# The third token tiles of the last two halves multiplied by the output weights as one pair, by Strassen's algorithm

## The chip, the cores and the metric

One core of a Trainium2 chip runs the whole program. The metric is the device time of one execution in microseconds. The kernel before takes 241.07 us as the median of three runs (240.97 to 242.35).

The engines are named as in the profile: PE (TensorE, matrix products; PEld is its loading of weights), DVE (VectorE), ACT (ScalarE), POOL (GpSimd) and SP (SyncE, which here only issues transfers). PE writes its results into eight PSUM banks; DVE and ACT read them out.

## The reference

Attention over 4 batches, 8 heads, 768 positions and 64 numbers per head, with a window of 96 positions, 8 global positions and a bias by distance, and then a feed-forward network with a gate on the 3072 tokens:

```python
scores = scale * q @ k^T + bias;  scores = where(keep, scores, -1e9)
a = exp(scores - max);  a = a / (sum(a) + 1e-09)
x = (a @ v), heads side by side                      # 3072 x 512
gate = maximum(x @ w_gate, 0.0)                      # 512 x 1536
val = x @ w_val                                      # 512 x 1536
out = (gate * val) @ w_out                           # 1536 x 512, float32
```

The kernel computes in bfloat16 with sums in float32.

## The kernel before

The tokens are cut into eight halves, numbered 0 to 7: half a batch each, 384 tokens, as three tiles of 128. For half c the kernel does attention, which gives `xT` (512 x 384), and then the network. Attention of half c + 1 is interleaved with the network of half c, so half 7's network has nothing beside it.

The network of a half is made by `ffn_pieces(c)` as two lists of pieces, each with a weight (about its PE time in microseconds) that serves to space other work. The list `f1` holds 24 products: for each of 12 chunks of the 1536 columns a gate product (`gate`, L521) and a val product (`val`, L528), four matmuls of 384 columns each. ACT applies the maximum (`grelu`, L525) and DVE multiplies val by it into `ht` (L531). `ht` has two buffers, so that of half c stays whole until half c + 2 begins. The list `f2` holds the product with the output weights `wo_sb`. In every half from 1 on:

- The third tile of 128 tokens is multiplied directly (`outp`, L533 to L544): 12 matmuls of 512 columns in four parts of three, a copy by ACT (L543) into a staging tile `osb`, and a store on SP's queue.
- The first two tiles are multiplied together by Strassen's algorithm. Written as a 2 x 2 block matrix, rows being the two tiles and columns the two halves of the 1536 chunks, the left side is multiplied by the 2 x 2 blocks of `wo_sb` in seven products `p4, p3, p1, p2, p5, p6, p7` (in this order) in place of eight. Each product is six matmuls of 256 columns (`block`, L579). The sums of weight blocks are made once (`wo_sum`, L805). The sums of blocks of `ht` are made by DVE in each half: `sum_cb` (for p2 and p5), `sum_ad` (for p1) and `sum_de` (for p6 and p7). Parts of them follow the val products 2, 5, 8, 9 and 10; the last parts stand in `f2`, before its items 2, 3 and 5. The results are put together in the staging tiles: ACT copies p4, p3 and p1; DVE adds and subtracts p2 and p5 in two passes each (L611, L612, L616, L617); p6 and p7 accumulate in the banks of p3 and p1 and take one pass each (L624, L629). Half 7 stores its two tiles in four transfers of half a tile, the others in two whole ones.

The order of all instructions is written out by hand: each engine executes its own in program order. `weave(f_items, *placed)` (L664) issues the pieces of the network one after another and, after each, those other pieces whose place has been passed. `spread` (L659) gives the attention pieces places at equal distances between two fractions of the half's weight: from 0.0 to 0.8 in halves 3 to 6, from 0.07 to 0.82 in half 2, and the preparation of keys and queries of the half after that from 0.25 to 0.75. An attention piece is a group of score products (L397, with ACT's exponential L406 and DVE's masks L359), the product with the values for one head of a pair (`piece_av`, L416, with ACT's logarithm L436 and, after the second head, exponential L441), or the normalization of a pair into `xT` (`piece_norm`, L443, two DVE passes).

From half 1's end on the banks are in two pools: `ff` has three, taken in turn by gate and val products, by the plain tile and by p4, p3 and p1; `x` has five, taken by scores, value products, p2 and p5. A product whose bank has not been read out waits, and all that follows on PE waits with it. At the start of half c from 2 on, `begin` (L546) issues the first gate and val products together, in the order of the parts of `xT`.

Of the kernel before, what the change touches and what calls it, by code (L numbers as in the profile page):

```python
# [8 lines left out]
FP32 = mybir.dt.float32  # L9
BF16 = mybir.dt.bfloat16  # L10
AF = mybir.ActivationFunctionType
ALU = mybir.AluOpType
# [3 lines left out]
def kernel(  # L16
# [12 lines left out]
    nc = tc.nc  # L29
# [14 lines left out]
    NHALF = 2 * B  # L44
# [27 lines left out]
    late = {}  # L72

    PSUM = bass.MemoryType.PSUM
    psum = {}
# [20 lines left out]
    wo_sb = const.tile([128, N_FC, DM], BF16)  # L96
# [408 lines left out]
    out_v = out.rearrange("(s p n) d -> s n p d", p=128, n=NN)  # L505

    begin_of = {}

    def ffn_pieces(c):
        ht = ht_pool.tile([128, N_FC, QH], BF16, name="ht")  # L510
        st = {}
# [38 lines left out]
            if c == 2:  # L550
                product(wg, "g", 1, 0, N_DC - 1)


        N2, D2 = N_FC // 2, DM // 2
        tiles_ = [slice(n * 128, (n + 1) * 128) for n in range(2)]

        def sums_of(name, *shape):
            if name not in st:
                st[name] = late["sums"].tile([128, *shape], BF16, name=name)
            return st[name]  # L560

        cb = lambda: sums_of("cb", N2, 2, 128)
        ad = lambda: sums_of("ad", N2, 128)
        de = lambda: sums_of("de", N_FC, 128)

        def sum_cb(i0, i1):
            nc.vector.tensor_tensor(cb()[:, i0:i1].rearrange("f i n t -> f i (n t)"), ht[:, i0:i1, 0:256],
                                    ht[:, N2 + i0 : N2 + i1, 0:256], op=ALU.add)

        def sum_ad(i0, i1):  # L570
            nc.vector.tensor_tensor(ad()[:, i0:i1], ht[:, i0:i1, tiles_[0]],
                                    ht[:, N2 + i0 : N2 + i1, tiles_[1]], op=ALU.add)

        def sum_de(i0, i1):
            x, y = (1, 0) if i0 < N2 else (0, 1)
            nc.vector.tensor_tensor(de()[:, i0:i1], ht[:, i0:i1, tiles_[x]], ht[:, i0:i1, tiles_[y]],
                                    op=ALU.subtract)

        def block(key, pool, left, right, start, stop):  # L579
            if start:  # L580
                st[key] = psum[pool].tile([128, 512], FP32, name=f"{pool}_ps")
            for i in range(N2):
                nc.tensor.matmul(st[key][:, 0:D2], lhsT=left(i), rhs=right(i),  # L583
                                 start=start and i == 0, stop=stop and i == N2 - 1,
                                 skip_group_check=not start)
            return st[key][:, 0:D2]

        c0, c1 = slice(0, D2), slice(D2, DM)
        bs = lambda name: lambda i: late["bs"][name][:, i]
        V2 = nc.vector.tensor_tensor  # L590

        def store(n, cols, eng=nc.sync):
            eng.dma_start(out=out_v[c, n][:, cols], in_=st["r", n][:, cols])

        def p4():
            for n in range(2):
                st["r", n] = late["osb"].tile([128, DM], FP32, name="osb")
            ps = block("d", "ff", lambda i: ht[:, N2 + i, tiles_[1]], bs("b21-b11"), True, True)
            nc.scalar.copy(st["r", 0][:, c0], ps)

        def p3():
            ps = block("c", "ff", lambda i: ht[:, i, tiles_[0]], bs("b12-b22"), True, True)
            nc.scalar.copy(st["r", 0][:, c1], ps)

        def p1():
            ps = block("a", "ff", lambda i: ad()[:, i], bs("b11+b22"), True, True)
            nc.scalar.copy(st["r", 1][:, c1], ps)

        def p2():
            ps = block("b", "x", lambda i: cb()[:, i, 1], lambda i: wo_sb[:, i, c0], True, True)  # L610
            V2(st["r", 1][:, c0], ps, st["r", 0][:, c0], op=ALU.add)  # L611
            V2(st["r", 1][:, c1], st["r", 1][:, c1], ps, op=ALU.subtract)  # L612

        def p5():
            ps = block("e", "x", lambda i: cb()[:, i, 0], lambda i: wo_sb[:, N2 + i, c1], True, True)
            V2(st["r", 0][:, c1], ps, st["r", 0][:, c1], op=ALU.add)  # L616
            V2(st["r", 0][:, c0], st["r", 0][:, c0], ps, op=ALU.subtract)  # L617
            if c == NHALF - 1:
                store(1, c0)
                store(0, c1)  # L620

        def p6():
            ps = block("c", "ff", lambda i: de()[:, i], bs("b11+b12"), False, True)
            V2(st["r", 1][:, c1], ps, st["r", 1][:, c1], op=ALU.add)  # L624
            store(1, slice(0, DM) if c < NHALF - 1 else c1, nc.sync if c < NHALF - 1 else nc.scalar)

        def p7():
            ps = block("a", "ff", lambda i: de()[:, N2 + i], bs("b21+b22"), False, True)
            V2(st["r", 0][:, c0], ps, st["r", 0][:, c0], op=ALU.add)  # L629
            store(0, slice(0, DM) if c < NHALF - 1 else c0)  # L630

        behind = {2: [lambda: sum_de(0, 3)], 5: [lambda: sum_de(3, 6)], 8: [lambda: sum_cb(0, 3)],
                  9: [lambda: sum_ad(0, 3)], 10: [lambda: sum_de(6, 9)]}

        def val_and_sums(fc):
            val(fc)
            for f in behind.get(fc, ()):
                f()

        begin_of[c] = (begin, lambda: gate(0, N_DC - 1), lambda: val(0, N_DC - 1))  # L640
        f1 = []
        for fc in range(N_FC):
            f1.append((0.65, lambda fc=fc: gate(fc)))
            f1.append((0.65, lambda fc=fc: (val if c < 1 else val_and_sums)(fc)))
        f2 = [(0.65, lambda n=n, part=part: outp(n, part))
              for n in (range(NN) if c < 1 else (NN - 1,)) for part in range(4)]
        if c >= 2:
            f1[:2] = [(1.0, begin_of[c][0]), (0.15, begin_of[c][1]), (0.15, begin_of[c][2])]
        if c == 2:
            f1[0] = (1.5, f1[0][1])  # L650
            f1[3] = (0.15, lambda: gate(1, N_DC - 1))
        if c >= 1:
            f2 += [(0.65, f) for f in (p4, p3, p1, p2, p5, p6, p7)]
            for at, f in ((5, lambda: sum_de(9, 12)), (3, lambda: sum_cb(3, 6)), (2, lambda: sum_ad(3, 6))):
                f2.insert(at, (0.0, f))
        return f1, f2

# [98 lines left out]
    pool = ctx.enter_context(tc.tile_pool(name="late0", bufs=1, side="right", reuse_waits="tile"))  # L756
# [25 lines left out]
    for f in ("m1 g0 m3 v0 m2 g1 K3 K2 m0 g3 K1 S30 S31 g2 K0 S20 v3 S11 v1 S21 A3 N3 v2 S00 S01 "  # L782
              "g5 A2 S10 g4 g6 A0 N2 v5 v4 N0 A1 N1 g7 v7 v6").split():
        i = int(f[1])
# [8 lines left out]
        else:  # L793
# [3 lines left out]
    early.close()  # L797
    ctx.enter_context(open_psum(ff=3, x=5))
    pool = ctx.enter_context(tc.tile_pool(name="late", bufs=1, reuse_waits="tile"))
    late["osb"] = ctx.enter_context(tc.tile_pool(name="osb", bufs=3, reuse_waits="tile"))  # L800
    late["sums"] = ctx.enter_context(tc.tile_pool(name="sums", bufs=1, reuse_waits="tile"))
    late["bs"] = {name: pool.tile([128, N_FC // 2, DM // 2], BF16, name=f"bs{i}")
                  for i, name in enumerate(("b21-b11", "b12-b22", "b11+b22", "b11+b12", "b21+b22"))}

# [39 lines left out]


# [33 lines left out]
```

## Time and profile before

| | |
|---|---|
| median of three runs | 241.07 us (240.97 to 242.35) |
| the profiled execution's own time | 241.74 us |
| its span, from the first to the last instruction | 239.9 us |
| granted TensorE clock, mean | 0.998 |
| PE busy | 233.5 us, 1937 matmuls |
| DVE busy | 173.3 us |
| ACT busy | 153.4 us |
| POOL busy | 85.9 us |
| gate and val products (L518) | 160.9 us of PE |
| plain products with `wo_sb` (L538) | 29.6 us of PE, 112 matmuls of 512 columns |
| network of half 7, its first product to the last pass | 213.69 to 237.08 us |

How to read it: the profile is one execution. "Busy" is the sum of the instructions' lengths in which an engine is at work; matmuls overlap each other, so the distance between the starts of two of them is the time that one takes from PE. In a timeline a line gives the start, the length, the engine, the source line, the operation, output and inputs, the number of instructions that are merged, and in brackets the engine's idle time before them and what ended it.

### The profile page before, as it was taken

The numbers are of one execution on the slowest core, as the hardware profiler recorded it, in microseconds if no ns is written. First come the engines' busy times: TensorE is split into PE (matmuls) and PEld (weight loads), VectorE is DVE, ScalarE is ACT, GpSimd is POOL, SyncE is SP. The second block draws the span as 40 slices with busy tenths as digits, with TensorE's granted clock in tenths as the row PEclk, the third lists the DMA queues.
The fourth block names the chain that finished last, engine by engine and source line by source line (L and its number), as shares of the span: only waits on it lengthen the run. The fifth ranks groups of instructions, "written<-read, shape, count | busy, mean of one in ns | idle before, by whom it ended". The sixth has DMA issues, their size and how long they took to land.

```text
span 239.9 us, 5355 instructions
## 1 busy us (share of the span) xinstructions
PE 233.5 (97%) x1937; PEld 146.6 (61%) x1945; DVE 173.3 (72%) x456; ACT 153.4 (64%) x347; POOL 85.9 (36%) x202
## 2 busy tenths in 40 slices
PE   7899999999999999999999999999999999999994
PEld 3655555665458566666668566676658566676663
DVE  7775955869677788777787687866887677764643
ACT  5897883337775777748774777638774677733330
POOL 6767893208414860903274060902350000000000
PEclk9999999999999999999999999999999999999999
DMA  6999999993976997098519939398431200030003
GB/s 200 181 198 177 257 234 219 185 162 61 270 178 134 301 150 131 8 185 257 108 25 122 285 93 133 19 166 262 67 68 44 90 0 0 3 129 3 4 27 104
DMA packets 69603, 31.42 MB, mean 131 GB/s; under 512 B 47160, under 2 KB 66616, under 8 KB 69576
## 3 DMA queue, kind: packets, MB, share of 16 engines
q0 software_dynamic: 31744, 8.71, 35.3%
q1 hardware_dynamic: 36616, 21.45, 35.1%
q10 hardware_dynamic: 1216, 0.92, 1.2%
q8 instruction: 15, 0.25, 0.4%
q14 instruction: 12, 0.10, 0.1%
HBM read 28.41 MB, written 6.29 MB: 145 GB/s over the span
## 4 chain that ended last, share of the span: by engine, by line
PE 91%; ACT 3%; DVE 2%; issue 1%; ACTq 0%
PE ff_ps L518 53%; PE ff_ps L538 9%; PE ff_ps L583 8%; PE x_ps L427 6%; PE x_ps L397 4%; PE x_ps L583 3%; PE t_ps L459 2%; PE s_ps L341 2%; PE t_ps L272 1%; PE t_ps L682 1%; ACT lnd L436 1%; PE t_ps L310 1%; DVE xT L446 1%; PE s_ps L321 1%; ACT rcp L441 0%
## 5 line engine op out<-in xcount | busy, mean ns | idle before, releaser
L518 PE MATMUL ff_ps<-xT,wg 128*128 128x384 bf16 x384 | 80.7, 326 | 0.5 <-ACT grelu L525 0.4
L518 PE MATMUL ff_ps<-xT,wv 128*128 128x384 bf16 x384 | 80.2, 326 | 0.0
L531 DVE TENSOR_TENSOR ht<-ff_ps,grelu 128x384 bf16<-128x384 f32 x96 | 53.1, 554 | 28.5 <-PE ff_ps L518 13.8
L525 ACT ACTIVATE grelu<-ff_ps 128x384 bf16<-128x384 f32 x96 | 47.1, 492 | 39.4 <-PE ff_ps L518 20.9
L518 PEld LDWEIGHTS <-wg 128*128 128x128 bf16 x384 | 35.9, 98 | 23.9 <-issue 0.9
L518 PEld LDWEIGHTS <-wv 128*128 128x128 bf16 x384 | 36.1, 97 | 23.4 <-issue 1.2
L406 ACT ACTIVATE es<-x_ps 128x360 bf16<-128x360 f32 (+2 forms) x96 | 36.8, 444 | 16.9 <-PE x_ps L397 16.8
L359 DVE TENSOR_TENSOR es<-es,m_all 128x432 bf16<-128x432 bf16 (+4 forms) x108 | 31.2, 334 | 8.2 <-ACT es L406 7.8
L446 DVE TENSOR_TENSOR xT<-x_ps,rcp 64x384 bf16<-64x384 f32 x48 | 26.6, 554 | 9.4 <-ACT rcp L441 8.8
L436 ACT ACTIVATE lnd<-x_ps 64x384 f32<-64x384 f32 x48 | 23.3, 485 | 12.5 <-PE x_ps L427 11.8
L538 PE MATMUL ff_ps<-wo_sb,ht 128*128 128x512 bf16 x112 | 29.6, 379 | 0.4
L363 POOL CAST kqc<-ks 128x384 bf16<-128x384 f32 x24 | 11.6, 532 | 32.3 <-DMA ks<-in_k_dram 32.3
L137 POOL DMA_DIRECT2D vbuf<-in_v_dram x25 | 21.6, 880 | 2.6 <-DMA wv<-in_moe_w_val_dram 2.1
L427 PE MATMUL x_ps<-es,vbuf 128*128 128x216 bf16 (+4 forms) x216 | 21.8, 225 | 0.0
L427 PEld LDWEIGHTS <-vbuf 128*128 128x128 bf16 x216 | 15.8, 97 | 7.7
L538 PEld LDWEIGHTS <-ht 128*128 128x128 bf16 x120 | 10.8, 97 | 9.8 <-issue 0.2
L263 POOL COPY kT<-kqT 128x240 bf16<-128x240 bf16 x16 | 6.9, 430 | 23.0 <-DMA kqT<-kqc 20.5
L363 POOL CAST kqc<-qs 128x384 bf16<-128x384 f32 x24 | 11.6, 522 | 8.1 <-DMA qs<-in_q_dram 8.1
L259 POOL COPY kT<-kqT 128x360 bf16<-128x360 bf16 x10 | 6.0, 604 | 19.9 <-DMA kqT<-kqc 19.9
L441 ACT ACTIVATE rcp<-lnd 128x384 f32<-128x384 f32 x24 | 12.6, 524 | 0.7
L347 ACT ACTIVATE ef<-s_ps 128x720 bf16<-128x720 f32 (+2 forms) x16 | 10.9, 710 | 2.1 <-PE s_ps L341 1.8
L397 PE MATMUL x_ps<-kqT,kT 64*128 64x216 bf16 (+4 forms) x216 | 11.8, 224 | 0.2
(115 smaller groups left out, 252.8 us busy)
## 6 DMA issues: line engine op xcount, KB each, us to landing
out_dram<-osb SPq DMA_DIRECT2D x22, 256.0 KB, 2.7
ks<-in_k_dram SPq DMA_DIRECT2D x6, 768.0 KB, 5.5
qs<-in_q_dram SPq DMA_DIRECT2D x6, 768.0 KB, 12.1
vbuf<-in_v_dram POOLq DMA_DIRECT2D x21, 120.0 KB, 7.9
wg<-in_moe_w_gate_dram POOLq DMA_DIRECT2D x3, 512.0 KB, 7.9
wv<-in_moe_w_val_dram POOLq DMA_DIRECT2D x3, 512.0 KB, 9.8
wo_sb<-in_moe_w_out_dram POOLq DMA_DIRECT2D x1, 1536.0 KB, 19.6
kq<-in_q_dram ACTq DMA_DIRECT2D x2, 192.0 KB, 4.7
```

The costliest lines, as they stand in the source:

```text
L137: nc.gpsimd.dma_start(out=v_dst(b, NG + r0, NG + r0 + n, j), in_=v[b, :, KT * j + r0 : KT * j + r0 + n, :].rearrange("h p d -> p h d"))
L359: nc.vector.tensor_mul(for_all, for_all, mk)
L363: nc.gpsimd.tensor_copy(kqc[:, :, i].rearrange("t n (h d) -> t h n d", d=D)[:, 2 * p : 2 * p + 2], of[s][:, 2 * p : 2 * p + 2, :].rearrang ...
L406: nc.scalar.activation(es[:, e, 0:c], banks[e][:, 0:c], AF.Exp, bias=0.0, scale=scale)
L427: nc.tensor.matmul(av3[:, :, a : a + w], lhsT=vb[:, j, z0 : z0 + 128], rhs=es[:, e, c : c + NN * w].rearrange("k (n p) -> k n p", n=NN), s ...
L436: nc.scalar.activation(ln[o0 : o0 + 64], av[d0 : d0 + 64, 0:QH], AF.Ln, bias=0.0, scale=1.0)
L446: nc.vector.tensor_tensor(xT_of[s][r, p, :], av_of[s, p, e][r, 0:QH], av_of[s, p, "r"][r], op=ALU.mult)
L518: nc.tensor.matmul(st[key][:, 0:QH], lhsT=w_of(w, dc, fc), rhs=xT_of[c][:, dc, :], start=(dc == 0), stop=(dc == N_DC - 1))
L525: nc.scalar.activation(gr, psg[:, 0:QH], AF.Relu, bias=0.0, scale=1.0)
L531: nc.vector.tensor_tensor(ht[:, fc, :], psv[:, 0:QH], st["gr", fc], op=ALU.mult)
L538: nc.tensor.matmul(ps2, lhsT=ht[:, fc, n * 128 : (n + 1) * 128], rhs=wo_sb[:, fc, :], start=(fc == 0), stop=(fc == N_FC - 1))
L583: nc.tensor.matmul(st[key][:, 0:D2], lhsT=left(i), rhs=right(i), start=start and i == 0, stop=stop and i == N2 - 1, skip_group_check=not s ...
```

## The change

The functions of the Strassen product move out of `ffn_pieces` into `strassen(pair, sums)`, which takes any two tiles, each given as half, `ht` and tile number, and the pool for the sums of blocks. Halves 6 and 7 no longer multiply their third tile directly. Half 7 multiplies its own third tile and that of half 6 as one pair, with the tile of half 7 as the first; these seven products stand between half 7's last val product and its old pair. The sums for the new pair come from a pool of their own, `sums3`: `cb3(1)` follows val product 1 of half 7, `ad3` product 6, the first half of `de3` product 7, and `cb3(0)` and the second half of `de3` stand in `f2`.

In half 6 `f2` begins with p4, and the last sums stand before its items 0, 1 and 2; in half 7 the five remaining sums stand before items 0 to 4. The new pair is stored with two whole transfers on SP's queue. The pool of staging tiles has four instead of three.

The fractions for `spread` are multiplied by `part`, which is 22.6 over the half's weight: 22.6 / 22.75 in halves 2 to 5, 22.6 / 20.15 in half 6. The pieces of a half are made before the loads for the half two later are issued.

In the order of instructions this means, besides the new products: in halves 3 to 6 the value product of the second head of pair 2 (and what ACT does with it) comes before the gate product of chunk 11 instead of after it; in half 2 the attention pieces from the masks after pair 1's second score group up to pair 2's value products each come one product earlier. POOL's and SP's orders stay, but for the two stores.

```diff
+    def strassen(pair, sums):
+        N2, D2 = N_FC // 2, DM // 2
+        st = {}
+        last = pair[0][0] == NHALF - 1 and pair[0][2] == 0
+        def h(i, f0, f1):
+            _, ht, n = pair[i]
+            return ht[:, f0:f1, n * 128 : (n + 1) * 128]
...
+        def sum_cb_of(i):
+            V2(cb()[:, :, i], h(i, 0, N2), h(i, N2, N_FC), op=ALU.add)
+        def sum_ad(i0, i1):
+            V2(ad()[:, i0:i1], h(0, i0, i1), h(1, N2 + i0, N2 + i1), op=ALU.add)
+        def sum_de(i0, i1):
+            x, y = (1, 0) if i0 < N2 else (0, 1)
+            V2(de()[:, i0:i1], h(x, i0, i1), h(y, i0, i1), op=ALU.subtract)
...
+        def p4():
+            for i in range(2):
+                st["r", i] = late["osb"].tile([128, DM], FP32, name="osb")
+            ps = block("d", "ff", lambda i: h(1, N2 + i, N2 + i + 1)[:, 0], bs("b21-b11"), True, True)
+            nc.scalar.copy(st["r", 0][:, c0], ps)
...
+        return sum_cb, sum_cb_of, sum_ad, sum_de, [(0.65, f) for f in (p4, p3, p1, p2, p5, p6, p7)]
+    PAIRED = (6,)
+    third_of = {}
...
+        plain = range(NN) if c < 1 else () if c - c % 2 in PAIRED else (NN - 1,)
+        sum_cb, _, sum_ad, sum_de, products = strassen([(c, ht, 0), (c, ht, 1)], "sums")
         behind = {2: [lambda: sum_de(0, 3)], 5: [lambda: sum_de(3, 6)], 8: [lambda: sum_cb(0, 3)],
                   9: [lambda: sum_ad(0, 3)], 10: [lambda: sum_de(6, 9)]}
+        rest = (lambda: sum_ad(3, 6), lambda: sum_cb(3, 6), lambda: sum_de(9, 12))
+        if c in PAIRED:
+            third_of[c] = ht
+        elif c - 1 in PAIRED:
+            _, cb3, ad3, de3, products3 = strassen([(c, ht, NN - 1), (c - 1, third_of[c - 1], NN - 1)], "sums3")
+            behind[1] = [lambda: cb3(1)]
+            behind[6] = [lambda: ad3(0, N_FC // 2)]
+            behind[7] = [lambda: de3(0, N_FC // 2)]
+            rest = (lambda: cb3(0), lambda: de3(N_FC // 2, N_FC)) + rest
...
         if c >= 1:
-            f2 += [(0.65, f) for f in (p4, p3, p1, p2, p5, p6, p7)]
-            for at, f in ((5, lambda: sum_de(9, 12)), (3, lambda: sum_cb(3, 6)), (2, lambda: sum_ad(3, 6))):
+            f2 += (products3 if c - 1 in PAIRED else []) + products
+            places = (2, 3, 5) if plain else (0, 1, 2) if c in PAIRED else (0, 1, 2, 3, 4)
+            for at, f in list(zip(places, rest))[::-1]:
                 f2.insert(at, (0.0, f))
...
-    late["osb"] = ctx.enter_context(tc.tile_pool(name="osb", bufs=3, reuse_waits="tile"))
+    late["osb"] = ctx.enter_context(tc.tile_pool(name="osb", bufs=4, reuse_waits="tile"))
     late["sums"] = ctx.enter_context(tc.tile_pool(name="sums", bufs=1, reuse_waits="tile"))
+    late["sums3"] = ctx.enter_context(tc.tile_pool(name="sums3", bufs=1, reuse_waits="tile"))
...
     for c in range(2, NHALF):
+        f1, f2 = ffn_pieces(c)
+        part = 22.6 / sum(t for t, _ in f1 + f2)
...
-            placed.append(spread(attention_pieces(c + 1), *((0.07, 0.82) if c == 2 else (0.0, 0.8))))
+            placed.append(spread(attention_pieces(c + 1), *((0.07, 0.82 * part) if c == 2 else (0.0, 0.8 * part))))
...
-            placed.append(spread(early_pieces(c + 2), 0.25, 0.75))
-        f1, f2 = ffn_pieces(c)
+            placed.append(spread(early_pieces(c + 2), 0.25 * part, 0.75 * part))
         weave(f1 + f2, *placed)
```

More of the change, by code (lines that the diff above doesn't have):

```diff
@@ L507, with sums_of, sum_cb, block @@
     begin_of = {}
+    c0, c1 = slice(0, DM // 2), slice(DM // 2, DM)
+    V2 = nc.vector.tensor_tensor
+    def strassen(pair, sums):
[5 more added lines that the diff above has]
+            return ht[:, f0:f1, n * 128 : (n + 1) * 128]
+        def sums_of(name, *shape):
+            if name not in st:
+                st[name] = late[sums].tile([128, *shape], BF16, name=name)
+            return st[name]
+        cb = lambda: sums_of("cb", N2, 2, 128)
+        ad = lambda: sums_of("ad", N2, 128)
+        de = lambda: sums_of("de", N_FC, 128)
+        def sum_cb(i0, i1):
+            ht = pair[0][1]
+            V2(cb()[:, i0:i1].rearrange("f i n t -> f i (n t)"), ht[:, i0:i1, 0:256],
+               ht[:, N2 + i0 : N2 + i1, 0:256], op=ALU.add)
+        def sum_cb_of(i):
[5 more added lines that the diff above has]
+            V2(de()[:, i0:i1], h(x, i0, i1), h(y, i0, i1), op=ALU.subtract)
+        def block(key, pool, left, right, start, stop):
+            if start:
+                st[key] = psum[pool].tile([128, 512], FP32, name=f"{pool}_ps")
+            for i in range(N2):
+                nc.tensor.matmul(st[key][:, 0:D2], lhsT=left(i), rhs=right(i),
+                                 start=start and i == 0, stop=stop and i == N2 - 1,
+                                 skip_group_check=not start)
+            return st[key][:, 0:D2]
+        bs = lambda name: lambda i: late["bs"][name][:, i]
+        def store(i, cols, eng=nc.sync):
+            c, _, n = pair[i]
+            eng.dma_start(out=out_v[c, n][:, cols], in_=st["r", i][:, cols])
+        def p4():
[3 more added lines that the diff above has]
+            nc.scalar.copy(st["r", 0][:, c0], ps)
+        def p3():
+            ps = block("c", "ff", lambda i: h(0, i, i + 1)[:, 0], bs("b12-b22"), True, True)
+            nc.scalar.copy(st["r", 0][:, c1], ps)
+        def p1():
+            ps = block("a", "ff", lambda i: ad()[:, i], bs("b11+b22"), True, True)
+            nc.scalar.copy(st["r", 1][:, c1], ps)
+        def p2():
+            ps = block("b", "x", lambda i: cb()[:, i, 1], lambda i: wo_sb[:, i, c0], True, True)
+            V2(st["r", 1][:, c0], ps, st["r", 0][:, c0], op=ALU.add)
+            V2(st["r", 1][:, c1], st["r", 1][:, c1], ps, op=ALU.subtract)
+        def p5():
+            ps = block("e", "x", lambda i: cb()[:, i, 0], lambda i: wo_sb[:, N2 + i, c1], True, True)
+            V2(st["r", 0][:, c1], ps, st["r", 0][:, c1], op=ALU.add)
+            V2(st["r", 0][:, c0], st["r", 0][:, c0], ps, op=ALU.subtract)
+            if last:
+                store(1, c0)
+                store(0, c1)
+        def p6():
+            ps = block("c", "ff", lambda i: de()[:, i], bs("b11+b12"), False, True)
+            V2(st["r", 1][:, c1], ps, st["r", 1][:, c1], op=ALU.add)
+            store(1, c1 if last else slice(0, DM), nc.scalar if last else nc.sync)
+        def p7():
+            ps = block("a", "ff", lambda i: de()[:, N2 + i], bs("b21+b22"), False, True)
+            V2(st["r", 0][:, c0], ps, st["r", 0][:, c0], op=ALU.add)
+            store(0, c0 if last else slice(0, DM))
+        return sum_cb, sum_cb_of, sum_ad, sum_de, [(0.65, f) for f in (p4, p3, p1, p2, p5, p6, p7)]
@@ L551, in begin @@
                 product(wg, "g", 1, 0, N_DC - 1)
[L554 to L630, printed above, removed]
+        plain = range(NN) if c < 1 else () if c - c % 2 in PAIRED else (NN - 1,)
+        sum_cb, _, sum_ad, sum_de, products = strassen([(c, ht, 0), (c, ht, 1)], "sums")
         behind = {2: [lambda: sum_de(0, 3)], 5: [lambda: sum_de(3, 6)], 8: [lambda: sum_cb(0, 3)],
@@ L645, in ffn_pieces @@
         f2 = [(0.65, lambda n=n, part=part: outp(n, part))
-              for n in (range(NN) if c < 1 else (NN - 1,)) for part in range(4)]
+              for n in plain for part in range(4)]
         if c >= 2:
```

## The prediction, made before the changed kernel was run

> **What bounds the kernel now.** I read the page from the top. The first fence holds the span, the busy times and the chain that ended last, by engine and by line.
>
> ```profile
> span 239.9 us, 5355 instructions
> ...
> PE 233.5 (97%) x1937; PEld 146.6 (61%) x1945; DVE 173.3 (72%) x456; ACT 153.4 (64%) x347; POOL 85.9 (36%) x202
> ...
> PE 91%; ACT 3%; DVE 2%; issue 1%; ACTq 0%
> PE ff_ps L518 53%; PE ff_ps L538 9%; PE ff_ps L583 8%; PE x_ps L427 6%; PE x_ps L397 4%; PE x_ps L583 3%; PE t_ps L459 2%; PE s_ps L341 2%; PE t_ps L272 1%; PE t_ps L682 1%; ACT lnd L436 1%; PE t_ps L310 1%; DVE xT L446 1%; PE s_ps L321 1%; ACT rcp L441 0%
> ```
>
> PE is the bound: 97% busy, 91% of the chain. So a product that goes is worth its PE time, and a wait that PE gets is paid in full. VectorE (DVE) has 28% spare on the mean, but the change works on the ends of two halves, so next I read the timeline there. The end of the kernel (start, length, engine, line, operation, count):
>
> ```profile
> 229.28 2.75 PE L538 MATMUL ff_ps<-wo_sb,ht 128*128 128x512 bf16 x11
> ...
> 231.88 1.47 PE L583 MATMUL ff_ps<-bs,ht 128*128 128x256 bf16 x12
> ...
> 233.19 0.82 PE L583 MATMUL ff_ps<-bs,ad 128*128 128x256 bf16 x6
> ...
> 233.84 1.47 PE L583 MATMUL x_ps<-wo_sb,cb 128*128 128x256 bf16 x12
> ...
> 235.15 1.47 PE L583 MATMUL ff_ps<-bs,de 128*128 128x256 bf16 x12
> ...
> 236.66 0.42 DVE L629 TENSOR_TENSOR osb<-ff_ps,osb 128x256 f32<-128x256 f32 x1 [0.16 <-PE ff_ps L583]
> ```
>
> Lengths overlap; the distance between starts is the cost. A plain tile (12 matmuls of 512 columns; one record is missing) takes 231.88 - 229.28 = 2.60 us, 0.217 each. Six matmuls of 256 columns take 233.84 - 233.19 = 0.65 us, 0.109 each; a Strassen pair (seven such products) takes 4.58.
>
> The same place in half 6, with the other engines:
>
> ```profile
> 204.23 0.83 ACT L406 ACTIVATE es<-x_ps 128x360 bf16<-128x360 f32 x2
> ...
> 205.15 0.49 ACT L525 ACTIVATE grelu<-ff_ps 128x384 bf16<-128x384 f32 x1
> ...
> 205.25 0.81 PE L518 MATMUL ff_ps<-xT,wv 128*128 128x384 bf16 x4
> 205.66 0.48 ACT L436 ACTIVATE lnd<-x_ps 64x384 f32<-64x384 f32 x1
> ...
> 205.90 1.46 PE L538 MATMUL ff_ps<-wo_sb,ht 128*128 128x512 bf16 x5
> 206.17 0.56 DVE L531 TENSOR_TENSOR ht<-ff_ps,grelu 128x384 bf16<-128x384 f32 x1 [0.78 <-ACT lnd L436]
> 206.17 0.52 ACT L441 ACTIVATE rcp<-lnd 128x384 f32<-128x384 f32 x1
> 206.65 0.59 DVE L359 TENSOR_TENSOR es<-es,m_all 128x384 bf16<-128x384 bf16 x2
> ...
> 207.15 1.12 DVE L446 TENSOR_TENSOR xT<-x_ps,rcp 64x384 bf16<-64x384 f32 x2
> ...
> 208.30 0.36 DVE L571 TENSOR_TENSOR ad<-ht 128x384 bf16<-128x384 bf16 x1
> ...
> 208.58 0.55 DVE L567 TENSOR_TENSOR cb<-ht 128x768 bf16<-128x768 bf16 x1
> ...
> 213.31 0.42 DVE L624 TENSOR_TENSOR osb<-ff_ps,osb 128x256 f32<-128x256 f32 x1
> ...
> 214.01 0.49 PE L518 MATMUL ff_ps<-xT,wv 128*128 128x384 bf16 x2
> ```
>
> To see: the last chunk of ht (206.17 to 206.73) and both sums (to 209.13) are done before PE reaches the Strassen products at 209.10 to 211.7, because the plain tile stands in between (205.90 to 209.10, with two attention pieces of 0.31 each). The pass of p6 (213.31 to 213.73) frees the bank that half 7's first val product takes at 214.01: 0.3 us of slack. The plain tile is cover for DVE, and half 6 loses it.
>
> **Part 1, the arithmetic on PE.** Two plain tiles go: 205.90 to 209.10 less 0.62 of attention, 2.58, and 2.60. One Strassen pair comes: 4.58. Sum **-0.60 us**. That needs weight loads that stay hidden, 42 in place of 24 and 0.098 each: the row shows 12 loads and 12 matmuls in 1.31 us, so they are.
> The Trainium skill, "TensorE: Matmul & The Clock Gate", section "The mechanism", says the contrary in one place, that a weight load overlaps a running matmul only when the row groups differ; here all loads fill the whole array. By it the pair would cost 42 x 0.207 = 8.7 us against 24 x 0.315 = 7.6, +1.1 in place of -0.60; the 0.109 us between starts disagrees, and I keep the row.
>
> **Part 2, the end of half 6.** In the new order v11, the last val product, is followed at once by p4, whose sixth matmul reads the last chunk of ht. Also the factor on the attention positions moves one attention product (second head of pair 2) ahead of the last gate product, so ACT gets its logarithm and exponential ahead of the last grelu. I work it through from the rows' starts; PE is unchanged up to 205.90.
> - ACT: es to 205.06, logarithm to 205.57, exponential to 206.08, grelu to 206.57. Before, it was done at 205.64.
> - DVE: the last ht chunk then runs 206.60 to 207.15 instead of 206.17 to 206.73.
> - PE: p4's sixth matmul would start at 205.90 + 5 x 0.109 = 206.45; with 0.2 for the release and the load (an estimate) it starts at 207.35: **+0.90**. p3 ends at 208.11, attention at 208.42, p1 at 209.07, attention at 209.38.
> - DVE, in the new order and at the row's distances: masks to 207.65, ad to 207.93, normalization of pair 2 (1.15) to 209.08, cb to 209.63, de to 210.0. p2 wants cb's second half at 209.71 and gets it at 209.83: **+0.12**.
> - p2 ends at 210.16, its two DVE passes run to about 211.1; the normalization of pair 3 stands next in DVE's queue (1.13) to 212.2, the two passes of p5 to 212.9, that of p6 to 213.3. PE has finished p7 at 212.12 and half 7's first gate product at 212.45; the val product waits for the bank of p6 until about 213.35: **+0.90**.
> So half 7's first val product comes at 213.35 instead of 214.01, 0.66 earlier, where without stalls it would be 2.58 earlier. Stalls together **+1.92**. Bounds: 0.45 from below, if grelu keeps its old time: ht ends at 206.73 and p4 waits 0.45, while DVE's work from there to p6's pass, 6.2 us without a pause, ends at 212.4 and the bank is in time; 0 if PE reaches p4 that much later than I have it; and 2.6 if each of the three releases takes 0.2 more. I take 1.9, since every duration in the chain is from a row.
>
> **Part 3, the end of half 7.** Seven more products stand there: 9.16 in place of 2.60 + 4.58, +1.98; this is already in the sum of part 1. The first four read half 6's ht and sums made behind products 1, 6 and 7, so the last ht chunk has 2.6 us. The new sums are five, of 768 elements each; the nearest row, cb, is 0.55, bounds 0.36 and 1.12 (ad; the pair of normalizations). In half 7 DVE is busy 11.95 of 23.2 us and a chunk period of 1.30 us holds 0.56 + 0.55. At the tail cb3's first half is needed 2.6 us after v11 and comes at 1.4; p6' and p7' free their banks at about 4.9 and 5.3, wanted at 5.2 and 5.9. Cost 0, up to 0.5 if the sums take 1.12. ACT does three copies of 0.37 for the plain copy of 0.57, and idles here. The two whole stores go to SP's queue some 3 us ahead of the last three, about the 2.7 us in which such a store lands: 0, up to 0.3. The last pass and store stay as they are.
>
> **Part 4, the rest.** The fourth staging tile takes away a wait for a store's landing that no row shows: 0. In halves 3 to 5 the late grelu delays the last chunk by 0.4 to 0.6 us, under the cover of the plain tile: 0. In half 2 some fifteen attention pieces come one product (0.65) earlier; there one score group takes 0.67 at 87.98 where others take 0.48, a wait of 0.2 for a bank that may go, and new ones may come: -0.2 to +0.6, taken as 0. Moving the halves' piece construction ahead of the loads changes nothing in SP's or GpSimd's order: 0.
>
> **Sum.** -0.60 + 1.92 = +1.32 us. Against the profiled execution's own 241.74 (span 239.9 and 1.8 around it) this is 243.1; that execution lies 0.67 over the median 241.07, so for the median 242.4. About 1% is what a measurement of this kernel can tell from no change, and this is 0.55%.
>
> **Rivals.**
> - Gain kept: ACT or DVE reach the releases in time and only part 1 is left, -0.6 to +0.1: 240.5 to 241.2. For it: DVE's 28% spare. Against: p4's sixth matmul cannot start before the last ht chunk, and with the trace's own 206.73 it is late. The other side is decided at the val bank: under 0.6 us of stalls in all, the kernel is faster. 0.22.
> - More stalls: half 2's earlier pieces meet banks not yet free (three later score groups, 0.2 to 0.4 each) or the tail of half 7 falls behind (0.5 to 0.8), 0.5 to 1.6 on top of the forecast: 242.9 to 244.0. For it: 87.98. Against: the same pieces at the same distance in halves 3 to 5 show no such wait. 0.18.
> - The change does not do what it says: the pair is more PE time than two tiles, 244. Against: 0.109 and 0.217. 0.03, within the last.
>
> **How the numbers follow.** Forecast 0.60, its own range 241.4 to 243.1. With the rivals the range is 240.3 to 243.5, which leaves out the edges of both. Faster by over 1% (under 238.7) has no mechanism: 0.02. Slower by over 1% (over 243.5) is half of the second rival: 0.09. Within 1%: 0.89.
>
> **What the changed profile would show.** Right: an idle of about 0.9 us within or behind p4 in half 6, with the last ht as releaser; the val product of half 7 starting some 0.7 us before 214.01, after an idle released by p6's pass; no idle among half 7's fourteen products. Wrong: the first val at 211.5 (gain kept), or PE idle in half 2. Wrong altogether if the products' distance is not 0.109.

## The result, and the profile after

The changed kernel takes 243.71 us (median of six runs, 243.25 to 244.33), the kernel before 241.56 us (six runs, 240.97 to 242.35). The ratio is 1.009, with a 95% interval of 1.0067 to 1.0114, that is +1.6 to +2.75 us. The forecast was 242.4 us, +1.32 over the median of before as it was then known (241.07). The direction was right and the time lies 0.2 us above the range, which ended at 243.5.

The profiled execution after takes 244.33 us, 2.59 more than that of before, at the same mean clock (0.998). Its page, in the first lines and the chain that ended last:

```profile
span 242.6 us, 5413 instructions
...
PE 234.3 (97%) x1963; PEld 148.0 (61%) x1963; DVE 176.8 (73%) x467; ACT 153.1 (63%) x348; POOL 85.9 (35%) x202
...
PE 77%; DMA 8%; DVE 5%; ACT 5%; issue 2%; POOL 1%; ACTq 0%
PE ff_ps L614 48%; PE ff_ps L551 9%; PE ff_ps L634 6%; PE x_ps L427 5%; DMA wv<-in_moe_w_val_dram 4%; DMA wg<-in_moe_w_gate_dram 4%; PE x_ps L397 4%; PE x_ps L551 3%; ACT lnd L436 2%; DVE xT L446 1%; PE t_ps L711 1%; ACT grelu L621 1%; DVE ht L627 1%; ACT es L406 1%; PE t_ps L459 1%
```

PE's arithmetic went down and its busy time didn't (234.3 against 233.5): the trace of before lacks eight matmuls (L538 has 112 records of 120). So the busy time can't show a gain of 0.6 us; distances between starts can. The chain now has 5% each of DVE and ACT, and among its lines are `grelu` (L621) and `ht` (L627), which the lines listed before did not have. Its 8% of DMA lies ahead of 28.6 us, in the transfers of the first weights (`wv`, `wg`), of which more below.

The waits of PE and of its weight loads name some that the trace of before doesn't have (engine, waiting line, what it waited for: us in total, times, longest). First the weight loads:

```profile
PEld L551 <- DVE ht L627: 0.8, 1, 0.8
...
PEld L427 <- DVE es L359: 0.7, 3, 0.3
...
PEld L397 <- DVE xT L446: 0.3, 1, 0.3
```

Then PE itself:

```profile
PE ff_ps L614 <- DVE osb L591: 0.8, 1, 0.8
PE ff_ps L551 <- DVE ht L627: 0.5, 1, 0.5
```

The `ht` and `osb` lines are the two large stalls of the prediction's part 2. The three of L427 on `es` are not in the prediction; the one of L397 on `xT` lies in half 2, where it had allowed for one. The timeline of half 6's end after the change (start, length, engine, line, operation, count):

```profile
206.64 0.48 ACT L436 ACTIVATE lnd<-x_ps 64x384 f32<-64x384 f32 x1
...
207.46 0.71 PE L551 MATMUL ff_ps<-bs,ht 128*128 128x256 bf16 x5
207.58 0.47 ACT L621 ACTIVATE grelu<-ff_ps 128x384 bf16<-128x384 f32 x1
208.09 0.56 DVE L627 TENSOR_TENSOR ht<-ff_ps,grelu 128x384 bf16<-128x384 f32 x1 [1.14 <-ACT grelu L621]
...
208.70 0.94 PE L551 MATMUL ff_ps<-bs,ht 128*128 128x256 bf16 x7 [0.54 <-DVE ht L627]
...
212.08 1.47 PE L551 MATMUL ff_ps<-bs,de 128*128 128x256 bf16 x12
212.35 1.12 DVE L446 TENSOR_TENSOR xT<-x_ps,rcp 64x384 bf16<-64x384 f32 x2
...
214.17 0.42 DVE L591 TENSOR_TENSOR osb<-ff_ps,osb 128x256 f32<-128x256 f32 x1
...
214.64 0.48 PE L614 MATMUL ff_ps<-xT,wv 128*128 128x384 bf16 x2 [0.76 <-DVE osb L591]
```

To see: p4 starts at 207.46; its sixth matmul would start at 207.46 + 5 x 0.109 = 208.00 and starts at 208.70, after the last chunk of `ht` (208.09 to 208.65). Half 7's first val product could start 0.33 after its first gate product (213.39), at 213.72, and starts at 214.64: the pass of p6 (L591) that frees its bank stands in DVE's queue behind the normalization of 212.35 and p5's two passes. The end of the kernel:

```profile
229.91 1.47 PE L551 MATMUL ff_ps<-bs,ht 128*128 128x256 bf16 x12
...
234.49 1.47 PE L551 MATMUL ff_ps<-bs,ht 128*128 128x256 bf16 x12
...
237.77 1.47 PE L551 MATMUL ff_ps<-bs,de 128*128 128x256 bf16 x12
...
239.28 0.42 DVE L596 TENSOR_TENSOR osb<-ff_ps,osb 128x256 f32<-128x256 f32 x1 [0.16 <-PE ff_ps L551]
```

The two pairs follow each other at 4.58 us, without a wait.

Where the 2.6 us between the spans lie (239.94 and 242.56 us), from the starts of the same gate and val products in the two traces:

| stretch | after minus before, us |
|---|---|
| start to half 0's ninth product (a wait for the first weights) | +0.52 |
| half 2 | +0.20 |
| halves 3, 4, 5 | +0.27, +0.25, +0.31 |
| half 6 up to p4 (before: the plain tile's start) | 0.00 |
| from there to half 7's first val product: 7.18 against 8.11 | -0.93 |
| first val product to the last pass: 24.64 against 22.65 | +1.99 |
| behind the last pass | 0.0 |

The first row is not the change's: the profiled executions of eight kernels with the same start differ there by up to 1.64 us (below). Without it the rows give +2.1, which agrees with the difference of the medians, +2.15.

In these two traces 0.83 us come from halves 3 to 5, where the change does nothing but move places by 0.7%. Half 3 shows how. Before (timeline around its last products):

```profile
122.89 0.44 PE L427 MATMUL x_ps<-es,vbuf 128*128 128x216 bf16 x4
...
123.08 0.49 ACT L525 ACTIVATE grelu<-ff_ps 128x384 bf16<-128x384 f32 x1
...
123.60 0.48 ACT L436 ACTIVATE lnd<-x_ps 64x384 f32<-64x384 f32 x1
...
124.08 0.56 DVE L531 TENSOR_TENSOR ht<-ff_ps,grelu 128x384 bf16<-128x384 f32 x1 [0.74 <-ACT lnd L436]
...
124.55 0.64 DVE L359 TENSOR_TENSOR es<-es,m_all 128x432 bf16<-128x432 bf16 x2
...
125.10 0.43 PE L427 MATMUL x_ps<-es,vbuf 128*128 128x216 bf16 x4
...
125.38 0.81 PE L538 MATMUL ff_ps<-wo_sb,ht 128*128 128x512 bf16 x3
```

After:

```profile
122.95 0.43 PE L427 MATMUL x_ps<-es,vbuf 128*128 128x216 bf16 x4
...
123.74 0.48 ACT L436 ACTIVATE lnd<-x_ps 64x384 f32<-64x384 f32 x1
...
124.25 0.52 ACT L441 ACTIVATE rcp<-lnd 128x384 f32<-128x384 f32 x1
...
124.68 0.47 ACT L621 ACTIVATE grelu<-ff_ps 128x384 bf16<-128x384 f32 x1
...
125.19 0.56 DVE L627 TENSOR_TENSOR ht<-ff_ps,grelu 128x384 bf16<-128x384 f32 x1 [0.94 <-ACT grelu L621]
...
125.66 0.59 DVE L359 TENSOR_TENSOR es<-es,m_all 128x432 bf16<-128x432 bf16 x2
...
125.82 0.71 PE L427 MATMUL x_ps<-es,vbuf 128*128 128x216 bf16 x4
...
126.09 0.11 PEld L427 LDWEIGHTS <-vbuf 128*128 128x128 bf16 x2 [0.17 <-DVE es L359]
...
126.37 0.81 PE L634 MATMUL ff_ps<-wo_sb,ht 128*128 128x512 bf16 x3
```

To see: before, the last `grelu` runs at 123.08, ahead of the logarithm; after, the logarithm and the exponential (`rcp`) go first, and `grelu` runs at 124.68. The last chunk of `ht` comes at 125.19 instead of 124.08. The whole half starts 0.72 us later in the second trace (first gate product at 105.33 instead of 104.61), so the chunk itself is 0.39 late. The masks (`es`) of pair 3 stand behind it in DVE's queue. The value product that needs these masks stands inside the plain tile. Before, it went through without a wait (start 125.10, the plain tile goes on at 125.38: 0.28). After, it starts at 125.82 and the plain tile goes on at 126.37: 0.55, so +0.27. The plain tile covers the late chunk of `ht`, as predicted; it does not cover what is queued behind that chunk.

In half 2 a score group of pair 3 meets a bank whose two readers (the normalization of pair 1) have just begun. The timeline there, after:

```profile
93.47 1.13 DVE L446 TENSOR_TENSOR xT<-x_ps,rcp 64x384 bf16<-64x384 f32 x2
...
93.53 0.86 PE L397 MATMUL x_ps<-kqT,kT 64*128 64x216 bf16 x10
...
94.06 0.11 PEld L397 LDWEIGHTS <-kT 64*128 64x128 bf16 x3 [0.30 <-DVE xT L446]
```

The same group took 0.48 at 93.85 before; it takes 0.86 now. The group at 87.98, 0.67 before, takes 0.48 now. That is about +0.4 and -0.2, the half's +0.20. It is not clear of chance: with the old order half 2 takes 27.72 us in the trace of before and 27.96 in that of e3 (last section), and 27.91 here.

### The profile page after: what moved, and what is told of

It is laid out like the page before. It is cut to its first block, busy times and chain, and to the rows that moved or that the text cites. A ratio compares the mean times of both kernels' runs of the same rounds, so it can differ in the third digit from the quotient of the medians.

```text
span 242.6 us, 5413 instructions
## 1 busy us (share of the span) xinstructions
PE 234.3 (97%) x1963; PEld 148.0 (61%) x1963; DVE 176.8 (73%) x467; ACT 153.1 (63%) x348; POOL 85.9 (35%) x202
## 4 chain that ended last, share of the span: by engine, by line
PE 77%; DMA 8%; DVE 5%; ACT 5%; issue 2%; POOL 1%; ACTq 0%
PE ff_ps L614 48%; PE ff_ps L551 9%; PE ff_ps L634 6%; PE x_ps L427 5%; DMA wv<-in_moe_w_val_dram 4%; DMA wg<-in_moe_w_gate_dram 4%; PE x_ps L397 4%; PE x_ps L551 3%; ACT lnd L436 2%; DVE xT L446 1%; PE t_ps L711 1%; ACT grelu L621 1%; DVE ht L627 1%; ACT es L406 1%; PE t_ps L459 1%
## 5 line engine op out<-in xcount | busy, mean ns | idle before, releaser
L627 DVE TENSOR_TENSOR ht<-ff_ps,grelu 128x384 bf16<-128x384 f32 x96 | 53.2, 555 | 29.3 <-PE ff_ps L614 12.7
L621 ACT ACTIVATE grelu<-ff_ps 128x384 bf16<-128x384 f32 x96 | 47.1, 492 | 39.4 <-PE ff_ps L614 19.9
L359 DVE TENSOR_TENSOR es<-es,m_all 128x432 bf16<-128x432 bf16 (+4 forms) x108 | 30.4, 328 | 8.2 <-ACT es L406 7.8
L634 PE MATMUL ff_ps<-wo_sb,ht 128*128 128x512 bf16 x96 | 24.2, 379 | 0.0
L427 PE MATMUL x_ps<-es,vbuf 128*128 128x216 bf16 (+4 forms) x216 | 22.4, 225 | 0.2
L427 PEld LDWEIGHTS <-vbuf 128*128 128x128 bf16 x216 | 15.9, 97 | 7.9 <-DVE es L359 0.7
L634 PEld LDWEIGHTS <-ht 128*128 128x128 bf16 x96 | 8.6, 97 | 7.9 <-issue 0.2
L551 PE MATMUL ff_ps<-bs,ht 128*128 128x256 bf16 x96 | 12.0, 273 | 0.5 <-DVE ht L627 0.5
L259 POOL COPY kT<-kqT 128x360 bf16<-128x360 bf16 x10 | 5.5, 554 | 19.0 <-DMA kqT<-kqc 19.0
```

What stands on the lines that cost most here:

```text
L359: nc.vector.tensor_mul(for_all, for_all, mk)
L427: nc.tensor.matmul(av3[:, :, a : a + w], lhsT=vb[:, j, z0 : z0 + 128], rhs=es[:, e, c : c + NN * w].rearrange("k (n p) -> k n p", n=NN), s ...
L621: nc.scalar.activation(gr, psg[:, 0:QH], AF.Relu, bias=0.0, scale=1.0)
L627: nc.vector.tensor_tensor(ht[:, fc, :], psv[:, 0:QH], st["gr", fc], op=ALU.mult)
L634: nc.tensor.matmul(ps2, lhsT=ht[:, fc, n * 128 : (n + 1) * 128], rhs=wo_sb[:, fc, :], start=(fc == 0), stop=(fc == N_FC - 1))
```

## The experiments

Two questions were open. Is it the shifted places alone that cost time in halves 2 to 5, and by which engine? And what sets the stalls at the end of half 6: the late chunk of `ht`, or DVE's queue? The kernel before was run beside them: 241.53 us (median of 27 runs) beside the first four, 241.52 (29 runs) beside the last four.

| kernel | median us | ratio to before, 95% |
|---|---|---|
| changed kernel | 243.71 | 1.009 (1.0067 to 1.0114) |
| e1_new_places_only | 242.53 | 1.0046 (1.003 to 1.0063) |
| e2_old_places | 242.21 | 1.0038 (1.0023 to 1.0053) |
| e3_p3_first | 242.27 | 1.0027 (1.0011 to 1.0042) |
| e4_norm_last | 241.34 | 0.9999 (0.9983 to 1.0015) |
| e5_late_log | 241.71 | 1.0002 (0.999 to 1.0014) |
| e6_norm_only | 241.78 | 1.0007 (0.9995 to 1.0019) |
| e7_two_pairs | 242.28 | 1.003 (1.0017 to 1.0044) |
| e8_three_pairs | 242.97 | 1.0056 (1.0042 to 1.0071) |

For the kernels that differ at the end of half 6, the traces give these distances (us):

| kernel | half 6's first product with `wo_sb` or its sums, to half 7's first val product | from there to the last pass | sum, against before |
|---|---|---|---|
| before | 8.11 | 22.65 | 0 |
| changed kernel | 7.18 | 24.64 | +1.06 |
| e2_old_places | 6.82 | 24.64 | +0.70 |
| e3_p3_first | 6.82 | 24.64 | +0.70 |
| e6_norm_only | 5.90 | 24.92 | +0.06 |
| e4_norm_last | 5.52 | 24.96 | -0.28 |

### The new places alone

The kernel before with the new fractions and nothing else:

```diff
     for c in range(2, NHALF):
+        part = 22.6 / 22.75
...
-            placed.append(spread(attention_pieces(c + 1), *((0.07, 0.82) if c == 2 else (0.0, 0.8))))
+            placed.append(spread(attention_pieces(c + 1), *((0.07, 0.82 * part) if c == 2 else (0.0, 0.8 * part))))
...
-            placed.append(spread(early_pieces(c + 2), 0.25, 0.75))
+            placed.append(spread(early_pieces(c + 2), 0.25 * part, 0.75 * part))
```

> The kernel before, with one edit: the fractions of the attention places times 22.6/22.75, so that its order in halves 2 to 5 is that of the changed kernel; no new pair. Theory A (the places cost time by themselves: in each half the late grelu delays the last ht chunk, DVE's masks queue behind it, and the value product of the last pair waits for them, 0.27 us a half in halves 3 to 6, and 0.2 in half 2): +1.3 us over the kernel before. Theory B (the places are harmless, the whole loss is at the ends of halves 6 and 7 and in memory layout or startup): 0.

Measured: 242.53 us, ratio 1.0046 (1.003 to 1.0063), +1.0 us by the medians. In the trace half 2 is 0.20 longer, halves 3, 4 and 5 are longer by 0.28, 0.41 and 0.27, and half 6, which keeps its plain tile here, by 0.22. The three waits of the value product's weight loads on the masks are there again (0.8 us in total). The stretches add up to 1.4, more than the medians show; half 4's part is 0.41 here and 0.25 in the changed kernel, whose order there is the same. So about half of the loss needs no Strassen product at all.

### The old places in the changed kernel

```diff
-        part = 22.6 / sum(t for t, _ in f1 + f2)
+        part = 22.74 / sum(t for t, _ in f1 + f2)
```

> The changed kernel with 22.74 for 22.6, so that its order up to half 6's last val product is that of the kernel before; the new pair stays. Theory A: halves 2 to 5 fall back to the times of before and the last ht chunk of half 6 comes 0.4 us earlier, so +0.7 us over the kernel before in place of the changed kernel's +2.15. Theory B: only half 6 gains by the earlier chunk, some 0.4, so +1.7.

Measured: 242.21 us, ratio 1.0038 (1.0023 to 1.0053). Halves 2, 3 and 5 take their old time, half 4 0.16 us less, and what is left, +0.70 in the table of distances, is the end of half 6 against the arithmetic. With `grelu` back at its old place p4's wait shrinks from 0.70 to 0.34 (sixth matmul at 207.78, p4 from 206.90). The wait for p6's bank stays at 0.92 (half 7's first gate product at 212.47, its first val product at 213.72 instead of 0.33 after it). So that wait does not come from the late chunk of `ht`.

### p3 ahead of p4

e2 with the first two products of half 6's pair exchanged, in the same banks. p3 reads the first six chunks of `ht`, so the last chunk gets 0.65 us more.

```diff
-            if start:
+            if start and key not in st:
...
+        def p4_tiles():
+            for i in range(2):
+                st["r", i] = late["osb"].tile([128, DM], FP32, name="osb")
+            st["d"] = psum["ff"].tile([128, 512], FP32, name="ff_ps")
...
+            (lambda: (p4_tiles(), p3()), p4, p1, p2, p5, p6, p7) if pair[0][0] in PAIRED else
+            (p4, p3, p1, p2, p5, p6, p7))]
```

> As the run with the old places, and in half 6 p3 is multiplied before p4, into the same banks as before, so that the last ht chunk is needed 0.65 us later. Theory A1 (behind the wait in p4 stands DVE's queue, which sets when half 7's first val product gets its bank): the wait in p4 goes, but comes back at p2 or at the bank; +0.7, no gain over the run with the old places. Theory A2 (each wait is paid by itself): the 0.4 us of p4's wait is gained, +0.3.

Measured: 242.27 us, ratio 1.0027 (1.0011 to 1.0042), and in the trace the same 6.82 us as e2. p4's wait is gone, and p2 waits in its place. The timeline (the first two lines are p2, the last is half 7's first val product):

```profile
208.98 0.49 PE L551 MATMUL x_ps<-wo_sb,cb 128*128 128x256 bf16 x3
...
209.68 1.16 PE L551 MATMUL x_ps<-wo_sb,cb 128*128 128x256 bf16 x9 [0.20 <-DVE cb L534]
...
213.23 0.48 PE L621 MATMUL ff_ps<-xT,wv 128*128 128x384 bf16 x2 [0.76 <-DVE osb L596]
```

p2's fourth matmul would start at 208.98 + 3 x 0.109 = 209.31 and starts at 209.68: 0.37 late, as much as p4 had been in e2 (0.34 there, 0.03 at p2). So the waits ahead of p2 don't add up. DVE's queue decides when p2 can run, and a product moved ahead of it only moves the idle time. The bank wait did not change.

### DVE's order at the end of half 6

e3 with the second half of `cb` ahead of pair 2's normalization, and pair 3's normalization behind the pass of p6:

```diff
-        N = lambda p: [(0.0, lambda: piece_norm(s, p))]
+        N = lambda p: [(0.0, lambda: piece_norm(s, p) if s - 1 not in PAIRED or p < HP - 1 else None)]
...
-            places = (2, 3, 5) if plain else (0, 1, 2) if c in PAIRED else (0, 1, 2, 3, 4)
+            places = (2, 3, 5) if plain else (0, 0, 2) if c in PAIRED else (0, 1, 2, 3, 4)
...
+        if c in PAIRED:
+            f2.insert(-1, (0.0, lambda: piece_norm(c + 1, HP - 1)))
```

> As the run with p3 first, and in half 6 DVE's order is changed: the last cb sum before the normalization of pair 2, and the normalization of pair 3 behind the pass of p6 instead of before the passes of p5. Theory A1 (DVE's queue, with the 1.1 us normalization in front of the pass that frees the bank, makes the wait of half 7's first val product): that wait goes to about 0.2 us, later at the last part of xT; -0.3 us against the kernel before. Theory A2 (the waits stand alone): the bank's wait of 0.8 goes, -0.4 against the kernel before; told from A1 by the run with p3 first. If neither moves the time, the loss isn't at this place: +0.7.

Measured: 241.34 us, ratio 0.9999 (0.9983 to 1.0015). It is 2.4 us under the changed kernel and can't be told from the kernel before. The timeline of the same place:

```profile
210.32 0.41 DVE L596 TENSOR_TENSOR osb<-ff_ps,osb 128x256 f32<-128x256 f32 x1
...
210.65 1.11 DVE L446 TENSOR_TENSOR xT<-x_ps,rcp 64x384 bf16<-64x384 f32 x2
210.65 0.49 PE L621 MATMUL ff_ps<-xT,wg 128*128 128x384 bf16 x2
...
210.98 0.49 PE L621 MATMUL ff_ps<-xT,wv 128*128 128x384 bf16 x2
...
211.82 0.32 PE L621 MATMUL ff_ps<-xT,wg 128*128 128x384 bf16 x1
...
212.27 0.81 PE L621 MATMUL ff_ps<-xT,wg 128*128 128x384 bf16 x4
```

The pass of p6 now runs at 210.32 and the val product follows its gate product at once. All stalls up to there are gone: 5.52 us, where the kernel before less the plain tile gives 8.11 - 2.58 = 5.53. Still the whole stretch is only 0.28 us shorter than before, not 0.60. The rest went into the first products of half 7. From the first val product to the next chunk's gate product (212.27) it takes 1.29 instead of 0.98 (214.01 to 214.99 before): the last part of `xT` is now made at 210.65 to 211.76, just when these products want it, and p7's pass stands behind it.

### The logarithm behind grelu

e1 (new places, plain tiles) with ACT's order alone put back: the logarithm and exponential of pair 2's second head are issued behind the last `grelu`. PE and DVE keep e1's order.

```diff
+        if p == 3 and g == 2 and s in later:
+            later.pop(s)()
...
+        def on_act():
+            nc.scalar.activation(ln[o0 : o0 + 64], av[d0 : d0 + 64, 0:QH], AF.Ln, bias=0.0, scale=1.0)
+            if e == 1:
+                av_inverse(s, p, ln)
+        if e == 1 and p == 2 and s >= 3:
+            later[s] = on_act
+        else:
+            on_act()
...
```

> As the run with the new places only, and ACT's logarithm and exponential for pair 2 (after its second value product) issued behind the last grelu, where they stood before; PE's and DVE's orders stay as with the new places. Theory A (the late grelu is the cause: chunk, masks, value product in turn): in halves 3 to 5 the 0.27 us a half and in half 6 as much go, and half 2's 0.2 stays: +0.2 us over the kernel before. Theory B (the earlier value product on PE costs by itself): +1.1 as with the new places.

Measured: 241.71 us, ratio 1.0002 (0.999 to 1.0014). Halves 3 to 6 take the old time again; half 2, where this edit leaves the order as it is in e1, keeps +0.20. No wait of a value product on masks is left. Half 3's timeline:

```profile
124.03 0.49 ACT L538 ACTIVATE grelu<-ff_ps 128x384 bf16<-128x384 f32 x1 [0.36 <-PE ff_ps L531]
...
124.54 0.48 ACT L439 ACTIVATE lnd<-x_ps 64x384 f32<-64x384 f32 x1
...
124.75 0.56 DVE L544 TENSOR_TENSOR ht<-ff_ps,grelu 128x384 bf16<-128x384 f32 x1 [0.66 <-PE ff_ps L531]
...
125.77 0.44 PE L429 MATMUL x_ps<-es,vbuf 128*128 128x216 bf16 x4
```

`grelu` is back ahead of the logarithm, `ht` comes 0.39 earlier than in the changed kernel (124.75 against 125.19, less the 0.05 by which half 3 starts earlier here), and the value product takes its 0.44 without a pause. This settles the cause in halves 3 to 5: two ACT instructions, 1.0 us long, ahead of one `grelu` cost a quarter to 0.4 of a microsecond in each half.

### The normalization alone

e2 with only pair 3's normalization moved behind the pass of p6; p4 stays first and `cb` where it was.

```diff
+        N = lambda p: [(0.0, lambda: piece_norm(s, p) if s - 1 not in PAIRED or p < HP - 1 else None)]
...
+        if c in PAIRED:
+            f2.insert(-1, (0.0, lambda: piece_norm(c + 1, HP - 1)))
```

> As the run with the old places, with one edit: the normalization of pair 3 in half 6 behind the pass of p6 on DVE. Theory A1: the 0.8 us wait of half 7's first val product goes, less 0.2 for the last part of xT, and p4's wait of 0.2 to 0.45 stays: +0.1 us over the kernel before. If the wait has another cause: +0.7 as with the old places.

Measured: 241.78 us, ratio 1.0007 (0.9995 to 1.0019). The bank wait is gone and p4's stays. The table of distances gives 0.92 less up to the first val product, and 0.28 given back in half 7, as in e4. So the bank wait was made by one normalization (two DVE passes, 1.11 us together) that stood ahead of the pass that frees the bank.

### More pairs

If the pair gains in e4's order, more third tiles might be joined: e4 with two pairs, and with three.

```diff
-    PAIRED = (6,)
+    PAIRED = (4, 6)
```

> As the run with the normalization last, with halves 4 and 5 paired too. If the arithmetic is worth 0.6 us a pair and the order at the end of an even half costs 0.3 of it: -0.5 us against the kernel before. Rival: half 5 has attention beside it, and its 14 products with five more sums and six more passes on DVE (about 4.9 us) make new waits: 0 to +0.5.

```diff
-    PAIRED = (4, 6)
+    PAIRED = (2, 4, 6)
```

> As before with halves 2 and 3 paired as well: by the arithmetic -0.8 us against the kernel before; by the rival +0.3 to +1.

Measured: 242.28 and 242.97 us, ratios 1.003 and 1.0056. Each further pair costs 0.7 to 0.95 us instead of gaining 0.6. The timeline of half 5's end in the kernel with two pairs:

```profile
181.15 1.12 DVE L446 TENSOR_TENSOR xT<-x_ps,rcp 64x384 bf16<-64x384 f32 x2
...
182.48 0.81 PE L551 MATMUL ff_ps<-bs,ht 128*128 128x256 bf16 x6 [0.46 <-ACT osb L571]
...
183.34 0.42 DVE L596 TENSOR_TENSOR osb<-ff_ps,osb 128x256 f32<-128x256 f32 x1
...
183.81 0.82 PE L551 MATMUL ff_ps<-bs,ad 128*128 128x256 bf16 x6 [0.52 <-DVE osb L596]
```

Fourteen products follow each other there with half 6's attention beside them. The second pair's p3 starts when ACT has copied p4 of the same pair (L571, 182.06 to 182.43), and its p1 when the pass of the first pair's p6 (L596) has freed a bank. From start to start, with 0.65 for a product, p3 is 0.63 late (its p4 starts at 181.20) and p1 0.68. A normalization stands ahead of the passes again. Half 7, which has no attention beside it, shows no such wait. Halves 4 and 5 together take 55.42 us, 0.73 more than in the kernel before; with the 0.60 that the pair saves, their stalls are 1.33, and these two make 1.31 of it. In the kernel with three pairs halves 4 and 5 take 0.78 more than before and halves 2 and 3 0.46; by which waits is open.

## Why the prediction was right and wrong

**The step that failed** is in part 4: "In halves 3 to 5 the late grelu delays the last chunk by 0.4 to 0.6 us, under the cover of the plain tile: 0." The late `grelu` was seen, and the size of its delay was right (0.39 us in half 3: 124.08 to 125.19, less the 0.72 by which the half starts later). What was not followed is who stands behind the late chunk on DVE: the masks of pair 3, and for these the value product in the middle of the plain tile. Measured +0.83 in three halves in place of 0 (0.69 to 1.09 against the traces of e2, e3, e4 and e6, which have the old order there). The new places alone cost it, and ACT's order alone takes it back. In half 6 the same late `grelu` was followed through every engine; in halves 3 to 5 it was stopped at the first cover, and the list of what the changed profile would show names no place there.

**Half 2**, also part 4: "-0.2 to +0.6, taken as 0". Measured +0.20, a difference that traces of the old order show among themselves (last section). Both parts that the sentence names came: the wait at 87.98 went, and a new one at 93.53 came. The rival "more stalls" had spoken of three later groups; there was one. Its other half, the tail of half 7, did not happen. That its amount came all the same (0.5 to 1.6 on top of the forecast; 0.83 measured) is luck: it came from halves 3 to 5, which the rival's argument against names as free of such a wait. That argument looked at banks, and the wait there was one for masks.

**Part 1** (-0.60) held: a pair takes 4.58 us and a weight load stays hidden (12 matmuls of 256 columns in 1.31 us, seven products after seven). e4 shows the 2.58 of the plain tile gone to within 0.01. The Trainium skill, "TensorE: Matmul & The Clock Gate", section "Back-to-back issue gap", gives 131 ns for sustained matmuls of 512 columns and calls N/2.4 + 2.5 ns, 216 at 512, too high for a stream; here a stream takes 0.217 us, the second figure. By the page's sustained figures two plain tiles would be 24 x 0.131 = 3.1 us and a pair at least 42 x 0.081 = 3.4 (an estimate with its figure for 128 columns), so that the pair could not have gained at all. The measurement decides: 5.18 us for the two tiles, 4.58 for the pair.

**Part 2** (+1.92) was right in mechanism and a little too large: 1.65. p4's sixth matmul waited 0.70 (predicted 0.90), p2 0.03 (0.12), the val product for p6's bank 0.92 (0.90). The 0.2 us that the sum gave to a release and a load was 0.05 (the chunk of `ht` ends at 208.65, the matmul starts at 208.70); that is most of the miss at p4. Its lower bound was wrong in a telling way. It took DVE's chain as one without a pause from the late `ht` to p6's pass, so that an earlier `grelu` would also end the bank wait. In e2 `grelu` had its old time, and the bank wait stayed at 0.92. The bound's own numbers do not add up to "in time" either: 206.73 and 6.2 make 212.93, and the val product, 0.45 late, would want the bank at 211.88. And DVE has a pause there: it idles 0.38 us before p2's first pass (211.68), since p2 has only begun at 210.74, and from p2 on the chain is two passes, the normalization of pair 3, two passes, the pass of p6. The normalization's place makes the wait, as e6 shows. Likewise the three stalls are not three independent terms: take p4's away and p2 gets it (e3).

The Trainium skill, "Perfetto Trace Analysis", section "Matmuls", advises that independent groups of matmuls go round different banks, so that one is read out while the next is computed. Here they do, and the pass that reads p6's bank takes 0.42 us; the trace adds that the reader's place in its own queue counts too, 0.92 us for 1.11 us of other work ahead of it.

**Part 3** held: +1.99 against +1.98, no wait among the fourteen products, and the stores at the end cost nothing. It was close at one place: p3 of the old pair starts at 235.15, and the pass that releases it ends at 235.14. (The new pair's p3 reads the first six chunks of half 7's own `ht`, not of half 6's; they are ready as early.) In part 4 the fourth staging tile shows in no wait.

**The sum.** The misses are +0.83 (halves 3 to 5), +0.20 (half 2), -0.27 (stalls) and +0.02, together +0.78; the measured difference of the medians, 2.15, lies 0.83 over the forecast's 1.32. That the predicted time is 1.3 low has a second cause: 0.49 is the base, whose median of three runs was 241.07 and of six 241.56. Either miss alone would have left the time inside the range (243.2 or 242.9, under 243.5).

**The rival "gain kept"** asked for under 0.6 us of stalls. With DVE's order changed too (e4) that condition is met, and 0.32 of the 0.60 still goes into the first products of half 7. The 0.28 that is left in the trace cannot be told from nothing in the times (0.9983 to 1.0015, or -0.4 to +0.4 us). So in e4's order the loss of the cover that the plain tile gave to DVE takes back about half of what the pair saves; in the changed kernel's order the stalls without it are 1.65.

## What to carry to other kernels

Follow a late instruction past the first cover, through everything that is queued behind it on its engine and the next, until PE is reached in every stage where it occurs; here the stage with the obvious cover cost 0.83 us. A saving of 0.6 us on the engine that is the bound is worth something only if the others can still deliver without the work that was taken out; look for long operations (1.1 us of normalization) in the queue ahead of short ones that free a bank (0.42 us). Test a change of placement by itself: a factor of 0.7% on the places of other work was about half of this change's loss, and one number undid it.

## What was not expected of the hardware

The wait for the first weights differs much between profiled executions whose start is the same program. Against the kernel before, half 0's ninth product came +0.52 us in the changed kernel and -0.46, +1.18, +0.53, -0.45, +0.44 and -0.35 in e1 to e6; in e2 PE alone waited 1.2 us for `wv`. A difference of 1 us between two profiled spans can be this alone, so the stretches were compared behind it.

Behind it, too, a half whose instructions stand in the same order can take up to 0.24 us more or less. With the old order half 2 takes 27.72 us in the kernel before and in e2, 27.92 in e4 and 27.96 in e3; half 4 takes 27.67 in the kernel before and 27.47 in e4; half 3 takes 26.91 or 26.92 in all of them. In half 2 it begins at DVE's sum `de` ahead of a normalization: 0.59 us in e3 (at 87.97), 0.36 in the kernel before (at 87.44). The normalization, and the score group that waits for it, come that much later. In e3 a cast of POOL is under way when the sum starts (from 86.49), in the kernel before it starts behind it (87.52). From half 2 on, in the traces from the kernel before to e6, 216 sums of this size (128 x 384, bfloat16) have no copy or cast of POOL beside them and take 0.35 to 0.36 us each; the 72 that have one take 0.35 to 0.73. No run changed POOL's work alone, so that it is the cause is not shown. A difference of 0.2 us in one half of one trace can be such chance; the +0.27 of half 3 is more than it, since the traces of the old order agree there to 0.01.
